# Seven block products for eight in a feature-axis transform: layer 1, blocks 0 to 2

## The chip, the cores and the metric

The kernel runs on one core of one Trainium2 chip. The metric is the device time of one execution in microseconds (us). Before the change it is 1423.32 us, the median of three runs that lie between 1423.19 and 1423.43.

The engines are named as in the profile: PE is the matrix engine (PEld its weight loads), DVE the vector engine, ACT the scalar engine, POOL the general one, and SP the engine that issues this kernel's DMAs. Each engine works through its own instructions in the order in which they were written, and waits where a semaphore is not there yet.

## The reference

Two layers, each an FNet mixing step and an MLP mixer block. x is 2048 by 512 in fp32, the MLP is 1376 wide.

```python
def _A_ref(x, dft_seq_re, dft_seq_im, dft_hid_re, dft_hid_im):
    a = jnp.einsum("bsd,ed->bse", x, dft_hid_re)
    b = jnp.einsum("bsd,ed->bse", x, dft_hid_im)
    return jnp.einsum("ts,bse->bte", dft_seq_re, a) - jnp.einsum("ts,bse->bte", dft_seq_im, b)
...
x = A_x
x = x + _A_ref(_layernorm(x, axis=-1), A_dft_seq_re, A_dft_seq_im, A_dft_hid_re, A_dft_hid_im)
x = x + _B_ref(_layernorm(x, axis=-1), B_w1, B_w2, B_w3, B_w4)
x = x + _A_ref(_layernorm(x, axis=-1), A_dft_seq_re, A_dft_seq_im, A_dft_hid_re, A_dft_hid_im)
x = x + _B_ref(_layernorm(x, axis=-1), B_w1, B_w2, B_w3, B_w4)
```

The change concerns the feature-axis transform (`dft_hid_re`, `dft_hid_im`) of the second `_A_ref`. The kernel does the two transforms in the other order: first along the sequence, then along the features.

## The kernel before, in words

Every product is made of three matmuls (`mm3`, L293 to L296). Each operand is split into a high part, which is its cast to fp32r (made by ACT), and a low part, which is what the cast lost (a subtraction on DVE). The three matmuls are high by high, high by low of the right operand, and low of the left operand by high. So the third matmul of a product is the first that needs the left operand's low part.

A mixing step goes through the 2048 rows in four blocks c = 0 to 3 of 512 rows (four tiles of 128). A block has two phases:

- `x_phase`, 16 steps. Step 2k ("plain") has 12 matmuls of 128x512 on a piece of the sequence matrix (`ws`, 512 KB), step 2k+1 ("one") has 6 on the difference of the piece's two halves. Called x0, x0', x1, x1', up to x7, x7' below.
- `y_phase`, 16 items of 12 matmuls each; each works on a sum of two pieces. Called y0 to y15 below.

What the sequence transform of a block yields (four tiles of 128x1024: re0, re1, im0, im1) needs a few sums and is then transformed along the features. For block c - 1 this happens inside the x phase of block c: eight calls of `hid`, 12 matmuls of 128x512 each, put before the steps that the table `HAT` names. The right operand of each is a 512 KB piece of the feature matrix (`hs`). `add_y` adds the sums from PSUM to the residual rows. The sums that come before (`im1-`, `re1+` and so on), and the highs and lows of the four tiles (`high`, `low`), stand in the table `late` and are issued at numbered steps of the x phase by `run_late`.

All right operands come through one stream. A piece is loaded by SP into one of four raw buffers (two more, when `state["wide"]` is set, for the pieces of a y phase: from x step 11 to the end of y). Then it becomes a slot of a ring of four: ACT casts the high part (L240, L243, L247), DVE subtracts for the low part (L257). A "one" step has a difference made on DVE first (L242), and a y item a sum (L246). A slot is made ahead, as soon as PE is done with the slot that stood in the same place. A raw buffer comes free as soon as ACT and DVE have read it, which is ahead of PE's use. The stream's loads, casts, lows and sums stand on each engine in the order of use, and between them stands what `late` and the hooks issue at the same step.

Ahead of layer 1 stands layer 0's MLP, which goes through two pairs of blocks (`by_pairs`). In the second pair (`pair == 1`, `next_too`; its main loop is at 614.7 to 687.0 us of the profile) a list `bg` of small steps is worked off by `one`, between the matmuls.

The functions that the change touches:

Of the kernel before, what the change touches and what calls it, by code (L numbers as in the profile page):

```python
# [13 lines left out]
P = 128  # L14
# [25 lines left out]
HORDER = ((1, 0), (0, 1), (1, 1), (0, 0))  # L40


@with_exitstack
def spectral_mlp_kernel(ctx: ExitStack, tc: tile.TileContext, x, ws, hs, w1, w2, w34, out):
# [17 lines left out]
    w3e = dram.tile([P, 2, CH], F32, name="w3e")  # L62
    w4s = [dram.tile([P, 4, 2, 2 * P], F32, name=f"w4s{i}") for i in range(NF // 2)]
# [39 lines left out]
    rr = [[re0[0], re1[0]], [im0[0], im1[0]]]  # L103
    rg = [[at(f"rg{i}{g}", RR + (4 * i + g) * 2 * CH, 2, CH) for g in range(KD)] for i in range(2)]
    ring, ringf = zip(*(both(f"ring{i}", RNG + i * 4 * CH, 2, 2, CH) for i in range(RING)))
    raw_at = [at(f"raw{i}", RAWS + i * 2 * CH, 2, CH, dtype=F32) for i in range(RAW)]
    raw_at += [at(f"raw{RAW + i}", word, 2, CH, dtype=F32) for i, word in enumerate((EXT + 4 * D, STG))]

# [52 lines left out]

    for layer in range(LAYERS):
        for c in range(NC):
# [29 lines left out]
    raws, slots, sums = {}, {}, {}  # L193
    held = {i: None for i in range(len(raw_at))}
    state = {"wide": False, "dma": 0, "one": 0, "two": 0, "use": 0, "made": 0, "done": 0, "limit": 0, "load": w_pieces[0]}
# [11 lines left out]
    def issue_dma(upto=None):  # L207
        while state["dma"] < (state["load"] if upto is None else upto):
# [12 lines left out]
            raws[i] = raw_at[r]  # L221
# [5 lines left out]
    def stage_one():  # L227
# [3 lines left out]
        issue_dma()  # L231
        if dest is None:
# [18 lines left out]
    def stage_two():  # L251
        n = state["two"]
        kind, ids, (a, b), _ = items[n]
        dest = slots[n]
# [6 lines left out]
    def room():  # L261
        n = state["one"]
        if n >= min(len(items), state["limit"]):
            return False
        if items[n][3] is not None:
# [16 lines left out]
    def stream():  # L282
# [150 lines left out]
    re0s, re1s, im0s, im1s = (f[:, :, 1] for _, f in (re0, re1, im0, im1))  # L433
    mid = [rr[i // 2][i % 2].rearrange("p t r (h d) -> p (t r h) d", h=2) for i in range(4)]
# [52 lines left out]
    def x_phase(c, hook):  # L487
        h = 0
        for k in range(NP):
            first, last = k == 0, k == NP - 1  # L490
            while c and h < NP and HAT[h] == k:
# [9 lines left out]
            hook(2 * k)  # L501
            mm_half(PC, ax[k][:, 2], s[:, 0], first, last)
            mm_half(PB, ax[k][:, 1], s[:, 1], first, last)
            if last:
                for i in range(2):
                    nc.scalar.copy(im1s[:, i], PC[i])
                for i in range(2):
                    nc.scalar.copy(re1s[:, i], PB[i])
            s = stream()
            run_late(2 * k + 1)  # L510
            hook(2 * k + 1)
            mm_half(PA, ax[k][:, 0], s[:, 0], first, last)
# [1419 lines left out]
```

## Time and profile before

| what | before |
|---|---|
| median of three runs | 1423.32 us |
| the profiled execution's own time | 1423.03 us |
| its span in the profile | 1421.1 us |
| PE busy | 1415.4 us |
| DVE busy | 1187.0 us |
| ACT busy | 743.0 us |
| mean DMA rate | 216 GB/s |
| x phase of layer 1, block 1 (times from the span's start) | 798.85 to 853.25 us |
| x phase of block 2 | 896.77 to 951.17 us |
| x phase of block 3 | 994.69 to 1049.09 us |

The span is the time that the profile's instructions cover. It is 1.9 us shorter than the execution's own time. PE's matmuls are pipelined: each takes 389 ns from start to end at 512 columns, but the next one starts 227 ns after it. So what counts on PE is the distance from start to start. A "busy" PE that is never idle can still be waited for by others; where PE itself waits, the profile lists it by line, with the engine that it waited for.

### The profile page before, as it was taken

The page shows a single profiled execution, that of the slowest core. Times are in us where ns is not written, and L with a number is a line of the kernel's source. Part 1 is how long each engine was busy: PE and PEld are TensorE (multiplying, and loading weights), DVE is VectorE, ACT ScalarE, POOL GpSimd, SP SyncE. Part 2 cuts the span into 40 slices and gives each one's busy share as a digit, 9 for nine tenths or more (in the row PEclk, how much of TensorE's full clock was granted, in tenths as well). Part 3 has the DMA queues.
Part 4 walks back from the last instruction along what each step waited for, and adds up shares of the span by engine and source line. Part 5 has one row for each costly group of instructions (what it writes and reads, how often), then busy time and mean ns, then how long its engine had stood idle before and what let it go on. Part 6 is the DMA issues. An engine that isn't in the chain of part 4 may idle for free.

```text
span 1421.1 us, 17861 instructions
## 1 busy us (share of the span) xinstructions
PE 1415.4 (100%) x6465; PEld 1180.1 (83%) x6465; DVE 1187.0 (84%) x1675; ACT 743.0 (52%) x1007; POOL 77.7 (5%) x105
## 2 busy tenths in 40 slices
PE   9999999999999999999999999999999999999998
PEld 7888888888888888888888888888888888899887
DVE  7986998988979888656789989889899788896676
ACT  6663464455566754434555544554555566453351
POOL 2100000000002000000000000000000020000000
PEclk9999999999999999999999999999999999999999
DMA  7867647659754857945556476575696456676864
GB/s 253 279 208 234 210 152 262 193 163 309 238 164 109 294 195 266 354 159 178 196 174 222 152 253 212 158 265 176 193 304 229 134 148 237 202 244 228 311 207 158
DMA packets 136488, 306.31 MB, mean 216 GB/s; under 512 B 9680, under 2 KB 58064, under 8 KB 133712
## 3 DMA queue, kind: packets, MB, share of 16 engines
q1 hardware_dynamic: 136400, 305.17, 65.1%
q8 instruction: 51, 0.84, 0.2%
q14 instruction: 37, 0.30, 0.1%
HBM read 250.87 MB, written 54.26 MB: 215 GB/s over the span
## 4 chain that ended last, share of the span: by engine, by line
PE 93%; DVE 4%; ACT 1%; issue 1%; POOL 0%; DMA 0%; DVEq 0%; ACTq 0%; POOLq 0%
PE psd L294 10%; PE psd L296 10%; PE psd L295 9%; PE psa L296 8%; PE psa L294 8%; PE psa L295 8%; PE psb L296 7%; PE psc L295 7%; PE psc L296 7%; PE psb L294 7%; PE psb L295 7%; PE psc L294 7%; DVE rest L480 0%; ACT tmp L342 0%; DVE ring L257 0%
## 5 line engine op out<-in xcount | busy, mean ns | idle before, releaser
L240 ACT CAST ring<-raw 128x1024 fp32r<-128x1024 f32 x127 | 133.3, 1054 | 78.5 <-PE psd L296 42.9
L257 DVE TENSOR_TENSOR ring<-raw,ring 128x1024 fp32r<-128x1024 f32 x126 | 153.5, 1220 | 13.1 <-ACT ring L240 13.0
L294 PE MATMUL psd<-ring,rr 128*128 128x512 f32 x208 | 80.9, 389 | 0.0
L295 PE MATMUL psd<-ring,rr 128*128 128x512 f32 x208 | 80.9, 389 | 0.0
L296 PE MATMUL psd<-ring,rr 128*128 128x512 f32 x208 | 80.9, 389 | 0.0
L334 POOL TENSOR_TENSOR rs<-ve,mhalf 128x4 f32<-128x4 f32 x16 | 26.9, 1683 | 723.8 <-DVE nm L333 723.8
L247 ACT CAST ring<-ring0f 128x1024 fp32r<-128x1024 f32 x28 | 29.6, 1057 | 50.7 <-DVE ring0f L246 50.7
L257 DVE TENSOR_TENSOR ring<-ring1f,ring 128x512 fp32r<-128x512 f32 (+1 forms) x56 | 53.3, 952 | 0.7 <-ACT ring L243 0.7
L313 POOL TENSOR_TENSOR rs<-ve,mhalf 128x2 f32<-128x2 f32 (+2 forms) x33 | 28.8, 872 | 415.7 <-DVE nb L312 415.7
L342 ACT ACTIVATE tmp<-xs,nb,rs 128x512 f32<-128x512 f32 x56 | 43.5, 814 | 14.6 <-POOL nb L314 14.6
L294 PE MATMUL psc<-ring,ay 128*128 128x512 f32 x128 | 49.8, 389 | 0.0
L295 PE MATMUL psc<-ring,ay 128*128 128x512 f32 x128 | 49.8, 389 | 0.0
L296 PE MATMUL psc<-ring,ay 128*128 128x512 f32 x128 | 49.8, 389 | 0.0
L294 PE MATMUL psb<-ring,ay 128*128 128x512 f32 x128 | 49.8, 389 | 0.0
L295 PE MATMUL psb<-ring,ay 128*128 128x512 f32 x128 | 49.8, 389 | 0.0
L296 PE MATMUL psb<-ring,ay 128*128 128x512 f32 x128 | 49.8, 389 | 0.0
L294 PE MATMUL psa<-ring,ay 128*128 128x512 f32 x126 | 49.0, 389 | 0.0
L295 PE MATMUL psa<-ring,ay 128*128 128x512 f32 x126 | 49.0, 389 | 0.0
L296 PE MATMUL psa<-ring,ay 128*128 128x512 f32 x126 | 49.0, 389 | 0.0
L294 PE MATMUL psd<-ring,ay 128*128 128x512 f32 x126 | 49.0, 389 | 0.0
L295 PE MATMUL psd<-ring,ay 128*128 128x512 f32 x126 | 49.0, 389 | 0.0
L296 PE MATMUL psd<-ring,ay 128*128 128x512 f32 x126 | 49.0, 389 | 0.0
(826 smaller groups left out, 4494.4 us busy)
## 6 DMA issues: line engine op xcount, KB each, us to landing
raw<-in_ws SPq DMA_DIRECT2D x183, 512.0 KB, 5.1
raw<-in_hs SPq DMA_DIRECT2D x56, 512.0 KB, 3.6
w4r<-w4d SPq DMA_DIRECT2D x44, 512.0 KB, 4.5
w3b<-w3d SPq DMA_DIRECT2D x10, 1792.0 KB, 8.9
w3d<-w3b SPq DMA_DIRECT2D x5, 1792.0 KB, 6.9
x1d<-tmp SPq DMA_DIRECT2D x12, 512.0 KB, 6.4
xs<-x1d SPq DMA_DIRECT2D x12, 512.0 KB, 5.0
w4d<-w4in SPq DMA_DIRECT2D x11, 512.0 KB, 4.7
```

The source lines that it names most:

```text
L240: nc.scalar.copy(dest[:, a:b, 0], r[0][:, a:b])
L247: nc.scalar.copy(dest[:, :, 0], lo)
L257: nc.vector.tensor_tensor(lo, src, hi.bitcast(F32), op=ALU.subtract)
L294: nc.tensor.matmul(o, lh, rh, start=first, stop=False, skip_group_check=more)
L295: nc.tensor.matmul(o, lh, rl, start=False, stop=False, skip_group_check=more)
L296: nc.tensor.matmul(o, ll, rh, start=False, stop=last, skip_group_check=more)
L313: nc.gpsimd.tensor_tensor(rs[:, :n], ve[:, :n], mhalf[:, 0, :n], op=ALU.pow)
L334: nc.gpsimd.tensor_tensor(rs, ve, mhalf[:, :, :2], op=ALU.pow)
L342: nc.scalar.activation(o, s, AF.Identity, bias=mr[2], scale=mr[1])
```

## The change

In layer 1, for blocks 0 to 2 (so in the x phases of blocks 1, 2 and 3), the feature transform is taken as a product of 2 by 2 blocks, and is done with seven block products for eight, in the manner of Strassen and Winograd. Each product (`hid7`) has 24 matmuls of 128x256 and stands before one of the steps of the new table `HAT7`. They are called h0 to h6 below, so h0 stands before x1', h1 before x2', h2 before x3', h3 before x4', h4 before x5, h5 before x6 and h6 before x7.

The left operands ("forms") are the tiles and four sums of them. Each form gets its high part by ACT into one of two places (`hf`) and its low part by DVE (`form_low`), at the step ahead of its product. `hid7_out` adds each product's result to the residual rows: six additions of 512 columns, and one of 1024. The eight casts and lows of `hs` pieces, and the four highs and lows of the tiles, go.

The right operands are seven forms of the feature matrix, the same for all blocks, 1 MB each in split form (2 pieces of 512 KB). They are made once, in layer 0's second MLP pair: `hs_forms` gives four quarters of steps (2 loads of 256 KB, then 4 sums, 7 casts, 7 lows and 7 stores of 256 KB each), which are zipped into `bg`. In layer 1 they are loaded into the raw buffers and used from there by PE with no further work. The entry "over" in `uses` says that such a buffer is free only when PE has used it. All six raw buffers are in use in these x phases too.

Besides: `w4_bring` loads into `w4_sumf`, since the sixth raw buffer's place is in use; the statistics of the rows (`y_stats`), their loads and stores are issued at other steps; in block 3 the transposes ahead of the MLP are issued later in the y phase.

```diff
+HAT7 = (3, 5, 7, 9, 10, 12, 14)
...
+    hsd = [[dram.tile([P, 2, CH], F32, name=f"hsd{i}{j}") for j in range(2)] for i in range(7)]
...
+    def form_items(step):
+        for h in range(7):
+            if HAT7[h] == step:
+                for j in range(2):
+                    item("form", piece(hsd[h][j]), dest=hsd)
+                    y_pieces.add(len(pieces) - 1)
...
             for k in range(NP):
-                if c:
+                if c and layer:
+                    form_items(2 * k)
+                elif c:
                     for h in range(NP):
                         if HAT[h] == k:
                             item("plain", piece(hs[HORDER[h % 4]]))
                 p = piece(ws[c, k][:, 2:4])
                 item("plain", p)
+                if c and layer:
+                    y_pieces.add(p)
+                    form_items(2 * k + 1)
                 item("one", p, span=(0, 1))
...
-            uses.setdefault(i, []).append((n, "two" if it[0] == "plain" else "one"))
+            uses.setdefault(i, []).append((n, {"plain": "two", "form": "over"}.get(it[0], "one")))
...
         if i and items[i - 1][3] is None:
             state["done"] += 1
-        state["use"] += 1
+        state.update(use=i + 1, over=i)
         prefetch()
         while state["two"] <= i:
             stage_two()
+        if items[i][0] == "form":
+            return raw_in[place[items[i][1][0]]]
         return slots.pop(i)
...
+    forms = [(a11, a11f), (a22, a22f), s2, (a21, a21f), s3, (a11, a11f), (a12, a12f)]
+
+    def form_high(n):
+        nc.scalar.copy(hf[n % 2], forms[n][1])
+
+    def form_low(n):
+        lo, src = forms[n]
+        nc.vector.tensor_tensor(lo, src, hf[n % 2].bitcast(F32), op=ALU.subtract)
...
+    def hid7(n):
+        ps, (lo, _) = PD[n % 2], forms[n]
+        new = n in (0, 1, 3, 6)
+        for h in range(2):
+            s = stream()
+            for i in range(2):
+                j = 2 * h + i
+                for q in range(2):
+                    v = slice(q * P, (q + 1) * P)
+                    first = new and not (j or q)
+                    o = ps[:, q * DH : (q + 1) * DH]
+                    mm3(o, hf[n % 2][:, j, v], lo[:, j, v], s[:, i, 0], s[:, i, 1], first, True, not first)
...
+        if tiles:
+            for i, f in (
+                (0, form_sum(im1s, im1s, re1s)),
+                (0, form_sum(im1s, im1s, X1, ALU.add)),
+                (1, lambda: form_high(0)),
+                (1, form_sum(s3[1], a11f, a21f)),
+                (2, lambda: form_low(0)),
+                (2, form_sum(re1s, re1s, t[:, 0:2], ALU.add)),
+                (3, form_sum(re0s, re0s, t[:, 0:2], ALU.add)),
+                (3, form_sum(re0s, re0s, t[:, 2:4], ALU.add)),
+                (4, lambda: form_high(1)),
+                (4, form_sum(s2[1], a22f, s3[1])),
+                (4, form_sum(a21f, a21f, a22f, ALU.add)),
+                (4, lambda: form_low(1)),
+                (5, lambda: form_high(2)),
+                (5, form_sum(a11f, a12f, s2[1])),
+                (6, lambda: form_low(2)),
...
+                (8, lambda: form_low(3)),
+                (8, lambda: form_high(4)),
+                (9, lambda: form_low(4)),
...
+                (13, lambda: form_low(6)),
+            ):
+                late.setdefault(i, []).append(f)
+            return
...
+            def out(i, n, src=None):
+                t, src = fp[i][0], raw[i] if src is None else src
+                act(t[:, :, 0], src)
+                nc.vector.tensor_tensor(t[:, :, 1], src, t[:, :, 0].bitcast(F32), op=ALU.subtract)
+                nc.sync.dma_start(places[n][0].rearrange("p i (l w) -> p i l w", l=2), t.bitcast(F32))
...
+                bg += [lows("t4"), *early]
+                bg[: len(work)] = [do_both(*fg) for fg in zip(bg, work)]
```

The order of the instructions shows what this does on two engines. First DVE, from the start of the x phase of block 1, before. The names: `rr11f` is im1, `rr01f` re1 and `rr00f` re0 (`rr11`, `rr01`, `rr00` their split forms), L480 is a sum, L441 a low of one of these tiles, L257 a low of a ring slot, L242 the difference for a "one" step.

```order
L480 TENSOR_TENSOR rr11f_167<-rr11f_167,rr01f_165 128x2x512
L257 TENSOR_TENSOR ring0_176<-raw3_187,ring0_176 128x2x512
L480 TENSOR_TENSOR rr01f_165<-rr01f_165,tmp_107 128x2x512
L242 TENSOR_TENSOR ring2f_181<-raw0_184 128x512
L257 TENSOR_TENSOR ring1_178<-raw0_184,ring1_178 128x2x512
L480 TENSOR_TENSOR rr11f_167<-rr11f_167,tmp_107 128x2x512
L441 TENSOR_TENSOR rr01_164<-rr01f_165,rr01_164 128x2x512
L257 TENSOR_TENSOR ring2_180<-ring2f_181,ring2_180 128x512
L257 TENSOR_TENSOR ring3_182<-raw1_185,ring3_182 128x2x512
L480 TENSOR_TENSOR rr00f_161<-rr00f_161,tmp_107 128x2x512
L441 TENSOR_TENSOR rr11_166<-rr11f_167,rr11_166 128x2x512
```

And the same place after the change. `imLf` holds im0 and im1, `reLf` re0 and re1; L552 is a sum, L479 the low part of a form, L285 a low of a ring slot, L266 the difference for a "one" step.

```order
L285 TENSOR_TENSOR ring0_200<-raw0_208,ring0_200 128x2x512
L552 TENSOR_TENSOR s3f_189<-imLf_183 128x1024
L266 TENSOR_TENSOR ring1f_203<-raw0_208 128x512
L479 TENSOR_TENSOR imL_182<-imLf_183,hf0_190 128x4x256
L552 TENSOR_TENSOR reLf_185<-reLf_185,tmp_121 128x1024
L285 TENSOR_TENSOR ring1_202<-ring1f_203,ring1_202 128x512
L285 TENSOR_TENSOR ring2_204<-raw1_209,ring2_204 128x2x512
L552 TENSOR_TENSOR reLf_185<-reLf_185,tmp_121 128x1024 x2
L266 TENSOR_TENSOR ring3f_207<-raw1_209 128x512
L552 TENSOR_TENSOR s2f_187<-reLf_185,s3f_189 128x1024
L552 TENSOR_TENSOR imLf_183<-imLf_183,reLf_185 128x4x256
L479 TENSOR_TENSOR reL_184<-reLf_185,hf1_191 128x4x256
```

Of the seven lows of forms, the first (`imL`, for h0) and the second (`reL`, for h1) stand here; ahead of the second stand all sums of the re tiles and two sums of forms (`s2f`, and the one into `imLf`), where before these tiles' sums and lows were spread over steps 1 to 6.

Second DVE, further on in the same x phase, after the change: from the low of x5 (from buffer `raw0`) on, with the lows for h3 (`imL`) and h4 (`s_`, here `s3`) and the low of x6 (from `raw1`).

```order
L285 TENSOR_TENSOR ring2_204<-raw0_208,ring2_204 128x2x512
L266 TENSOR_TENSOR ring3f_207<-raw0_208 128x512
L285 TENSOR_TENSOR ring3_206<-ring3f_207,ring3_206 128x512
L479 TENSOR_TENSOR imL_182<-imLf_183,hf1_191 128x4x256
L552 TENSOR_TENSOR tmp_121<-tmp_121,psd0_286 128x2x256
L285 TENSOR_TENSOR ring0_200<-raw1_209,ring0_200 128x2x512
L479 TENSOR_TENSOR s3_188<-s3f_189,hf0_190 128x1024
```

Before the change the same stretch, from the difference for x5' on, has no low of a left operand (the first row is the low of an `hs` piece, the others belong to x5, x5' and the next `hs` piece):

```order
L257 TENSOR_TENSOR ring3_182<-raw3_187,ring3_182 128x2x512
L242 TENSOR_TENSOR ring1f_179<-raw0_184 128x512
L257 TENSOR_TENSOR ring0_176<-raw0_184,ring0_176 128x2x512
L257 TENSOR_TENSOR ring1_178<-ring1f_179,ring1_178 128x512
L257 TENSOR_TENSOR ring2_180<-raw1_185,ring2_180 128x2x512
```

So the lows of h3 and h4 now stand behind the lows of the pieces x5 and x6 in DVE's order, although PE uses h3 ahead of x5 and h4 ahead of x5.

Third SP, the loads of the same stretch, before. What a row waits for stands behind it: `DVE_49` is a wait for DVE, `DMAHW` one for an earlier DMA.

```order
L222 DMA raw2_186<-in_hs 128x1024 [waits DMAHW2_49,DVE_49]
L222 DMA raw3_187<-in_hs 128x1024 [waits DMAHW3_49,DVE_49]
L222 DMA raw0_184<-in_ws 128x1024 [waits DMAHW5_49,DVE_49]
L222 DMA raw1_185<-in_hs 128x1024 [waits DMAHW6_49,DVE_49]
L222 DMA raw2_186<-in_hs 128x1024 [waits DMAHW4_49,DMAHW0_49,DVE_49]
```

And after. `rawr0` and `raw0` are one buffer under two names, and so for the others; `hsd30` and `hsd31` are the two pieces of h3, and so on; `PE_49` is a wait for PE.

```order
L243 DMA rawr1_215<-hsd30_95 128x1024 [waits DMAHW1_49,DMAHW2_49,DVE_49,Activation_49]
L243 DMA rawr4_218<-hsd31_96 128x1024 [waits PE_49]
L243 DMA rawr5_219<-hsd40_97 128x1024 [waits DMAHW3_49,PE_49]
L224 DMA tmp_121<-x2d_78 128x2x512 [waits DMAHW4_49]
L243 DMA rawr3_217<-hsd41_98 128x1024 [waits DMAHW0_49,DMAHW5_49,DVE_49,Activation_49]
L243 DMA raw0_208<-in_ws 128x1024 [waits DMAHW6_49,PE_49]
L243 DMA rawr2_216<-hsd50_99 128x1024 [waits DMAHW7_49,PE_49]
L243 DMA rawr0_214<-hsd51_100 128x1024 [waits DMAHW6_49,DVE_49,Activation_49]
L243 DMA raw1_209<-in_ws 128x1024 [waits DMAHW1_49,PE_49]
```

Here the load of x5 (`raw0`) waits for the last matmul of h2's first half, which reads `rawr0`, and that of x6 (`raw1`) for the last matmul of h3's first half, which reads `rawr1`. Before, no load of a piece for these x phases waited for PE. In the x phases of blocks 2 and 3 the buffers have other numbers, and x5 and x6 wait for the same two halves.

More of the change, by code (lines that the diff above doesn't have):

```diff
@@ L103, in spectral_mlp_kernel @@
     rr = [[re0[0], re1[0]], [im0[0], im1[0]]]
+    (imL, imLf), (reL, reLf) = (both(f"{n}L", RR + i * 4 * CH, 4, CH) for i, n in enumerate(("im", "re")))
+    s2, s3 = (both(f"s{n}", RR + word * CH, 4, DH) for n, word in ((2, 8), (3, 10)))
+    hf = [at(f"hf{i}", RR + (12 + 2 * i) * CH, 4, DH) for i in range(2)]
     rg = [[at(f"rg{i}{g}", RR + (4 * i + g) * 2 * CH, 2, CH) for g in range(KD)] for i in range(2)]
@@ L191, in spectral_mlp_kernel @@
         for i in it[1]:
-            uses.setdefault(i, []).append((n, "two" if it[0] == "plain" else "one"))
-    raws, slots, sums = {}, {}, {}
+            uses.setdefault(i, []).append((n, {"plain": "two", "form": "over"}.get(it[0], "one")))
+    raws, slots, sums, place = {}, {}, {}, {}
     held = {i: None for i in range(len(raw_at))}
-    state = {"wide": False, "dma": 0, "one": 0, "two": 0, "use": 0, "made": 0, "done": 0, "limit": 0, "load": w_pieces[0]}
+    state = {"wide": False, "dma": 0, "one": 0, "two": 0, "use": 0, "over": 0, "made": 0, "done": 0, "limit": 0, "load": w_pieces[0]}
     x_left = [(0, 1), (1, 1)] + [(j, 2) for j in range(2, NT, 2)]
@@ L231, in stage_one @@
         issue_dma()
+        if kind == "form":
+            state["one"] += 1
+            return
         if dest is None:
@@ L253, in stage_two @@
         kind, ids, (a, b), _ = items[n]
+        if kind == "form":
+            state["two"] += 1
+            issue_dma()
+            return
         dest = slots[n]
@@ L1835, in hook @@
                             f(7)
+                if layer and c:
+                    if k < 2:
+                        rows((pairs[1], X1)[k], x1d, (c - 1) * TC + (2, 0)[k], 2, False)
+                    if c < NC - 1:
+                        return
+                    if k in (0, 1):
+                        for j in (2 * k, 2 * k + 1):
+                            normed_act(tmp[:, j], xt(j), ln2[j])
+                    if k in (1, 2):
+                        for q in (2 * k - 2, 2 * k - 1):
+                            turn_one(turned0, q, tmp[:, q])
+                    if k == 3:
+                        turn_out(turned0)
+                    if k == NP - 1:
+                        turn_in(ztf[0])
+                    return
                 if k == 1 and c:
```

130 lines of the change are left out of this document (114 added, 16 removed).

## The prediction

> **What bounds the kernel now.** I read the page's busy times and PE's waits first.
>
> ```profile
> PE 1415.4 (100%) x6465; PEld 1180.1 (83%) x6465; DVE 1187.0 (84%) x1675; ACT 743.0 (52%) x1007; POOL 77.7 (5%) x105
> PE psd L139 <- POOL mhalf L55: 1.4, 1, 1.4
> PE psb L426 <- DVE rr L339: 0.2, 1, 0.2
> ```
>
> PE is busy for 1415.4 of 1421.1 us, and its two waits (the list of waits has no more) come to 1.6 us, the longest 1.4. So time goes only with PE's work, and every wait of PE is added whole. What a matmul costs is its distance to the next, which the view by windows gives: the three x phases of blocks 1 to 3, and a stretch of layer 1's MLP with nothing but matmuls of 256 columns (columns: window, its length, then busy time and count for PE, PEld, DVE, ACT, POOL).
>
> ```profile
> 798.85:853.25 54.40, 54.40 (x242) 45.05 (x240) 47.01 (x58) 26.90 (x32) 2.83 (x2) 1.00 0.69 229
> 896.77:951.17 54.40, 54.40 (x242) 45.05 (x240) 47.01 (x58) 26.90 (x32) 2.83 (x2) 1.00 0.70 229
> 994.69:1049.09 54.40, 54.40 (x242) 45.05 (x240) 47.02 (x58) 28.24 (x34) 2.83 (x2) 1.00 0.74 248
> 1255.20:1310.70 55.50, 55.50 (x469) 55.46 (x468) 45.32 (x65) 26.88 (x42) 0.00 (x0) 1.00 0.70 228
> L294 PE MATMUL psb<-un,hr 128*128 128x256 f32 x50 | 14.1, 283 | 0.0
> ```
>
> 54.40 us over 240 weight loads (one for each matmul; the window's edges cut two more matmuls) is 0.2267 us for 512 columns; 55.50 over 468 is 0.1186 for 256. The granted clock is 1.00 throughout.
>
> **What the seven products give.** A block had 8 x 12 = 96 matmuls, 96 x 0.2267 = 21.76 us. It now has 7 x 24 = 168 matmuls of half the width, 168 x 0.1186 = 19.92. That is 1.84 less for a block, 5.5 for three: 0.39%, no more, and only if PE waits for nothing new. The Trainium skill (TensorE: Matmul & The Clock Gate, Back-to-back issue gap) gives an isolated warm matmul N/2.4 + 2.5 ns, 215.8 and 109.2 here; by that the estimate would be 96 x 0.2158 - 168 x 0.1092 = 2.4 us a block. The trace's distances are longer at both widths, and decide.
>
> So what matters is whether the left operands' lows are there in time. I lay the rows of the changed order end to end with durations of this trace. DVE's at the start of block 1's x phase, with ACT's casts and two groups:
>
> ```profile
> 799.05 0.69 DVE L242 TENSOR_TENSOR ring3f<-raw 128x512 f32<-128x512 f32 x1 [1.31 <-PE psa L296]
> 802.90 1.22 DVE L257 TENSOR_TENSOR ring<-raw,ring 128x1024 fp32r<-128x1024 f32 x1 [0.28 <-ACT ring L240]
> 804.04 1.22 DVE L480 TENSOR_TENSOR rr01f<-rr01f,tmp 128x1024 f32<-128x1024 f32 x1
> 805.85 0.69 DVE L242 TENSOR_TENSOR ring2f<-raw 128x512 f32<-128x512 f32 x1 [0.59 <-PE psb L296]
> 806.46 1.22 DVE L257 TENSOR_TENSOR ring<-raw,ring 128x1024 fp32r<-128x1024 f32 x1
> 806.63 0.62 ACT L243 CAST ring<-ring2f 128x512 fp32r<-128x512 f32 x1 [0.28 <-DVE ring2f L242]
> L240 ACT CAST ring<-raw 128x1024 fp32r<-128x1024 f32 x14 | 14.7, 1054 | 10.5 <-PE psd L296 5.5 <-PE psb L296 3.6 <-ACT ring L240 1.2
> L296 PEld LDWEIGHTS psd<-ring,rr x32: 187/188/188, 807.2 to 844.6; 128*128 128x128 f32 x32
> L294 PE MATMUL psd<-ring,rr 128*128 128x512 f32 x32 | 12.4, 389 | 0.0
> ```
>
> A DVE row of 1024 elements takes 1.22 us, and the next starts 1.14 after it (802.90 to 804.04); one of 512 takes 0.69, the next 0.60 later (805.85 to 806.46). ACT's casts take 1.05 and 0.62; ACT starts 0.09 after DVE's end (805.85 + 0.69 to 806.63). A weight load is 0.19, and a matmul ends 0.39 - 0.23 = 0.16 after the next has started. DVE's waits for PE in these rows show that it already works at PE's heels here.
>
> **h0 and h1: DVE's queue.** Time 0 is the phase's start, 798.85. PE does x0 (12 matmuls, 2.72), x0' (1.36), x1 (2.72), then h0. Its third matmul is the first to read the low part: wanted at 6.80 + 2 x 0.12 = 7.04. DVE has, in order: the difference for x1' (starts 0.20), two sums of im1, low x1', low x2 (it needs x0's end on PE, then ACT's cast: 4.05, as at 802.90), s3, the difference for x2', low of h0. 4.05 + 1.14 + 1.14 + 0.60 = 6.93, plus 1.22 and the weight load: 8.34. PE waits 1.3 us. Then h1: PE goes on with 22 matmuls (2.61), x1' and x2 (4.08) and wants the low at 8.34 + 6.69 + 0.24 = 15.27. DVE, from 8.07: sum of re1, low x2', low x3, two sums of re0, difference for x3', s2, the sum into a21, low of h1; seven rows of 1.14 (the last ends 0.08 later) and two of 0.60 make 9.26 and end at 17.33, with the weight load 17.52. PE waits 2.25. Nothing covers this, since DVE has no gap there that the sums could use. Before, the same sums had up to twice the time, and lows of tiles were due later.
>
> **h2: 0.7.** The difference for x4' needs the ring place that x2' leaves (0.16), then 0.69, cast 0.62, low 0.60, the form's low 1.22, weight load 0.19 and hand-overs of 0.2: 3.7, against x3 and two matmuls (2.96).
>
> **h3 and h4: the raw buffers.** A form's buffer is freed by PE, not by DVE. The load of x5 waits for the end of h2's first half; the low of x5 stands ahead of the low of h3 on DVE; h3 comes ahead of x5 on PE. So between the end of h2's first half and h3's third matmul PE has only h2's second half 1.42, x3' 1.36, x4 2.72 and 0.24: 5.74 us. In that time must fit the landing L, cast 1.05, low x5 1.14, difference 0.69, cast 0.62, low x5' 0.60, h3's low 1.22, weight load 0.19, and hand-overs of 0.2: L + 5.7. PE waits L. For h4 it is the load of x6, freed by h3's first half, whose low stands ahead of h4's: L + 1.05 + 1.14 + 1.22 + 0.19 + 0.1 = L + 3.7, against 1.42 + 1.36 + 0.24 = 3.02: PE waits L + 0.7. Before, no such load waited for PE; SP's longest waits were for DVE. For L, the list of DMA issues and the view of the stream's line (all loads of the window 796 to 856):
>
> ```profile
> SPq L222 <- DVE ring L257: 37.9, 14, 5.6
> raw<-in_ws SPq DMA_DIRECT2D x183, 512.0 KB, 5.1
> raw<-in_hs SPq DMA_DIRECT2D x56, 512.0 KB, 3.6
> DMA to landing us min/median/max: 3.3/4.6/9.5
> ```
>
> I take 3.6, the row of the pieces that are loaded amid an x phase: these loads too start when little else is under way, since the queue behind them waits for PE. The bounds are 3.3 and 4.6. So h3 waits 3.6, h4 4.3.
>
> **h5, h6 and the y phase.** h5's low has 24 x 0.12 + 2.72 + 1.36 = 6.9 us after h4's and needs 0.69 + 0.62 + 0.60 for x6', 4 x 0.34 for a weight's sums, 0.60 for a result and 1.22: 5.1, so it costs nothing. h6's low stands behind y0's sum, which needs the ring place that x6 leaves: 0.16 + 1.14 + 1.22 + 0.19 = 2.7 against x6' and 0.24: 1.1. With L = 4.6 two loads one after the other (x7, then y0 in the same buffer) make 2 x 4.6 + 5.0 = 14.2, against 12.7 of PE: 1.5. In the y phases nothing is added between PE and its slots: 0, at most 0.5 in block 3, where DVE was busy for 42.8 of 43.6 us:
>
> ```profile
> 1049.00:1092.60 43.60, 43.60 (x194) 36.09 (x193) 42.81 (x41) 24.60 (x29) 0.00 (x0) 1.00 0.76 247
> ```
>
> **Layer 0's second pair.** It gains 44 DVE rows of 256 columns and 28 casts, and 28 stores and 8 loads of 256 KB.
>
> ```profile
> 614.70:687.00 72.30, 72.30 (x320) 59.89 (x319) 48.55 (x89) 33.99 (x53) 3.57 (x8) 1.00 0.44 150
> L480 DVE TENSOR_TENSOR w4sumf<-w4raw 128x256 f32<-128x256 f32 x2 | 0.8, 418 | 0.0
> ```
>
> DVE has 48.55 us of work in 72.30; 44 x 0.34 (0.42 less the overlap of 0.08) adds 15.0, which leaves 8.8 free, and ACT and the DMAs have half their time. The matmuls hide it: 0. If one step's seven rows end last somewhere, 7 x 0.42 = 2.9. It adds only, so no gain.
>
> **The sum.** A block: 1.3 + 2.25 + 0.7 + 3.6 + 4.3 + 1.1 = 13.25 of waits, less 1.84: 11.4. Blocks 1 to 3 have the same order and the same dependences: 34.2. On the profiled execution's 1423.0 (span 1421.1 and 1.9 around it; the median is 0.3 above): 1457.2, so 1457. With L = 3.3: 3 x 10.8 = 32.4, 1455; with L = 4.6: 3 x (15.6 - 1.8) = 41.5, plus 0.5 and 2.9: 1468.
>
> **The rivals.**
>
> *Only DVE's queue counts.* If the loads of x5 and x6 come early enough after all, h3 waits like h2 (0.7) and h4 not at all: 6.05 - 1.84 = 4.2 a block, 12.6 in all: 1435.6. If the short waits at h2, h3 and h6 vanish too (2.5 a block), 1428. For it: DVE's order needs no DMA to come out. Against it: the order's rows make those loads wait for PE. Chance 0.13.
>
> *All waits are covered, and it is faster.* DVE's total in an x phase hardly grows (it loses 12 lows of 1024 and four sums of 512, and gains 12 rows of 1024 and six of 512: 1.2 us of 54.4). If DVE did two of the sums before the phase's start, where it waits 1.31 us for PE (row 799.05), and came to h1 3.55 us sooner than I laid it, and the pieces x5 and x6 were in SBUF by then, PE would never wait: 1423.0 - 5.5 = 1417.5. It decides at h1: each us that is missing there costs 3, so with 1.8 us missing the gain is gone. Against it: DVE's rows have one order, and the sums stand behind the difference for x1', which waits for PE. Chance 0.07.
>
> *The clock falls in the long waits.* No wait of before is over 1.4 us, and there the granted clock stays 1.00; h3's and h4's would be 3.6 and 4.3. If matmuls after them ran at twice their distance for as long as one product (24 x 0.1186 = 2.85), six such waits add 17: 1474; four of the six, 1469. The Trainium skill (TensorE: Matmul & The Clock Gate, Part 1) has PE at half clock after an idle window of about 3.4 us, until it was busy for as long; by this the estimate is up to 1.7 us lost for each wait, 10 in all. It also has the window run freely, so that waits of 3.6 and 4.3 us would seldom cover a whole one. No run here shows it so far. Chance 0.10.
>
> **How the numbers follow.** Forecast 0.67 (1455 to 1468), only DVE's queue 0.13, faster 0.07, clock 0.10, and 0.03 that gain and waits cancel within 0.2% (2.8 us; less could hardly be told from no change). The range must take in the forecast with L's bounds and DVE's case, and the clock's lower part: 1428 to 1469. Faster 0.07, same 0.03, slower 0.90.
>
> **What would show it.** Right: PE's list of waits names the forms' lows (`imL`, `reL`, `s2`, `s3`), 11 to 15 us for each x phase of blocks 1 to 3 with the longest ahead of h4; these phases last some 65.8 us for 54.4; SP's loads of x5 and x6 wait for PE. Wrong: an x phase of about 52.6 us without waits of PE (faster), or one of 58.6 with waits at h0 and h1 alone. A granted clock under 1.00 in these phases is the third rival. PE's waits in layer 0's second pair should be none.

## The result, and the profile after

The changed kernel takes 1502.08 us (median of four runs, 1496.98 to 1503.56); the kernel before took 1423.26 beside it. The ratio is 1.0548 (95%: 1.0521 to 1.0574). The sign was as forecast, but the time lies outside the range. The profiled execution took 1500.71 us, its span is 1498.6: 77.5 us more than before. By stages (ends from the timeline of PE; the two profiled executions):

| stage | before | after | more |
|---|---|---|---|
| layer 0, second MLP pair | 107.60 | 126.28 | 18.7 |
| x phases of blocks 1, 2, 3 | 3 x 54.40 | 72.95, 70.78, 75.47 | 56.0 |
| y phases of blocks 1, 2 | 2 x 43.52 | 44.75, 44.77 | 2.5 |
| all else | | | 0.3 |

The page's busy times:

```profile
PE 1436.8 (96%) x6681; PEld 1200.9 (80%) x6681; DVE 1205.8 (80%) x1725; ACT 733.4 (49%) x1020; POOL 74.5 (5%) x105
```

PE's list of waits, without the two rows that stood there before (1.4 and 0.4 us here; columns: what waits and for whom; us in total, times, the longest):

```profile
PE psd L330 <- DVE s L479: 14.2, 6, 5.1
PE psd L330 <- DVE reL L479: 13.2, 6, 4.5
PE psd L330 <- DVE imL L479: 11.8, 6, 2.9
PE psd L328 <- ACT hf L475: 3.6, 6, 1.1
PE psa L328 <- DVE rest L552: 3.5, 2, 3.3
PE psd L328 <- DVE rest L552: 2.9, 2, 1.8
PE psd L328 <- ACT rest L1303: 2.0, 1, 2.0
PE psa L328 <- ACT rest L1303: 1.2, 1, 1.2
PE psd L330 <- DVE h L750: 1.2, 1, 1.2
PE psc L328 <- ACT h L760: 0.7, 1, 0.7
PE psd L328 <- DVE tmp L552: 1.9, 2, 0.9
```

The first four rows are the x phases: 42.8 us in 24 waits, for the forms' lows (L479) and highs (L475). L330 is the third matmul of a product, the one that the forecast named. The six rows below them are the second pair, 11.5 us in 8 waits, for sums and copies that empty PSUM banks. The last row is the y phases.

Waits don't carry all of it. The windows of the pair, of the three x phases, and of a stretch right behind the longest wait (columns as before: PE, PEld, DVE, ACT, POOL, then the granted clock):

```profile
615.00:741.30 126.30, 114.64 (x475) 91.42 (x474) 90.20 (x180) 58.82 (x106) 6.94 (x12) 0.96 0.65 223
817.80:890.75 72.95, 59.06 (x313) 51.24 (x312) 47.12 (x53) 23.36 (x29) 0.00 (x0) 0.93 0.61 198
935.50:1006.28 70.78, 57.97 (x313) 50.24 (x312) 47.12 (x53) 23.42 (x29) 0.00 (x0) 0.95 0.61 195
1051.05:1126.52 75.47, 59.38 (x313) 51.70 (x312) 47.11 (x53) 23.39 (x29) 0.00 (x0) 0.93 0.64 212
864.00:868.40 4.40, 4.40 (x22) 4.40 (x22) 3.63 (x8) 2.61 (x3) 0.00 (x0) 0.50 0.60 165
```

The 22 matmuls of the last window (two of them cut by its edges) start 0.21 us apart, for 0.1186 at full clock, and the clock column says 0.50. So the 56.0 us of the x phases are: 42.8 of waits, 24 x 0.16 = 3.8 because the last matmul ahead of a wait runs to its end, less 5.5 of gain; what is left, 14.9, is slower matmuls. Of these 10.9 stand in the timeline as matmuls at about twice their distance behind seven of the waits (1.2 to 2.4 us behind each); most of the rest is the first matmul after a wait, 0.10 longer to the next one than its neighbours. In the pair it is 11.5 of waits, 8 x 0.16 = 1.3, and 5.9 slower, 4.1 of them at twice the distance behind two waits (2.5 and 1.6).

How one wait comes about, h4 of block 1. PE's timeline (start, length; in brackets the idle time ahead of it), DVE's, SP's issues (a row's time is that of the first of the x issues in it), and ACT's row in its list of waits for the three blocks:

```profile
858.15 0.28 PE L329 MATMUL psd<-rawr,hf 128*128 128x256 f32 x1
863.57 0.58 PE L330 MATMUL psd<-rawr,s 128*128 128x256 f32 x1 [5.13 <-DVE s L479]
```

```profile
861.15 1.22 DVE L285 TENSOR_TENSOR ring<-raw,ring 128x1024 fp32r<-128x1024 f32 x1 [6.69 <-ACT ring L264]
862.29 1.22 DVE L479 TENSOR_TENSOR s<-s3f,hf 128x1024 fp32r<-128x1024 f32 x1
880.01 1.23 DVE L270 TENSOR_TENSOR ring0f<-raw,raw 128x1024 f32<-128x1024 f32 x1 [4.44 <-DMA raw<-in_ws]
881.16 1.22 DVE L479 TENSOR_TENSOR reL<-reLf,hf 128x1024 fp32r<-128x1024 f32 x1
```

```profile
855.40 0.33 SPq L243 DMA_DIRECT2D raw<-in_ws  x1
875.00 12.17 SPq L243 DMA_DIRECT2D raw<-in_ws  x7
```

```profile
ACT ring L264 <- DMA raw<-in_ws: 46.5, 9, 8.0
```

SP can issue the load of x6 only at 855.40, when PE has done with h3's first half, which lay in that buffer. ACT waits for the landing, DVE waits 6.69 us for ACT's cast, does the low of x6 at 861.15, and only then the low of h4 (862.29), which PE wants at 858.4. DVE had nothing to do in these 6.69 us but to hold its place in the queue. The same happens at h6: a load issued at 875.00 (just as DVE's low of x7 ends, at 874.98), a sum for y0 that waits for it until 880.01, and behind it the low of h6.

The second pair, where the forecast had no waits. SP's issues, then in the timelines DVE's first row of the forms' sums and one of ACT's casts, and the row of those casts in ACT's list of waits:

```profile
630.87 0.39 SPq L942 DMA_DIRECT2D w3b<-w3d  x1
631.31 0.42 SPq L1195 DMA_DIRECT2D hsr<-in_hs  x1
```

```profile
640.98 0.43 DVE L552 TENSOR_TENSOR hp01f<-hsr,hsm 128x256 f32<-128x256 f32 x1 [5.37 <-issue]
```

```profile
679.55 0.41 ACT L1199 CAST hp<-hsr 128x256 fp32r<-128x256 f32 x1 [5.50 <-DMA hsd<-hp]
```

```profile
ACT hp L1199 <- DMA hsd<-hp: 10.4, 5, 5.5
```

DVE waits 5.37 us at the head of its queue for a load of 256 KB that was issued right behind the 1.8 MB load of `w3b`; that small load landed 9.6 us after its issue. ACT waits five times, 10.4 us in all, for a store out of `hp` to be over before it may write `hp` again. Behind these rows stand the sums and copies that empty PE's PSUM banks.

### The profile page after: what moved, and what is told of

It reads as the page before. It is cut to its first block, busy times and chain, and to the rows that moved or that the text cites. A ratio compares the mean times of both kernels' runs of the same rounds, so it can differ in the third digit from the quotient of the medians.

```text
span 1498.6 us, 18501 instructions
## 1 busy us (share of the span) xinstructions
PE 1436.8 (96%) x6681; PEld 1200.9 (80%) x6681; DVE 1205.8 (80%) x1725; ACT 733.4 (49%) x1020; POOL 74.5 (5%) x105
## 4 chain that ended last, share of the span: by engine, by line
PE 81%; DVE 9%; DMA 5%; ACT 3%; issue 2%; SPq 0%; POOL 0%; DVEq 0%; ACTq 0%; POOLq 0%
PE psd L330 9%; PE psd L328 8%; PE psd L329 8%; PE psa L330 7%; PE psa L329 7%; PE psa L328 7%; PE psb L330 6%; PE psb L329 6%; PE psb L328 6%; PE psc L329 6%; PE psc L330 6%; PE psc L328 6%; DMA raw<-in_ws 3%; DVE ring L285 2%; DMA hsd<-hp 1%
## 5 line engine op out<-in xcount | busy, mean ns | idle before, releaser
L264 ACT CAST ring<-raw 128x1024 fp32r<-128x1024 f32 x103 | 107.9, 1051 | 108.6 <-DMA raw<-in_ws 48.5
L285 DVE TENSOR_TENSOR ring<-raw,ring 128x1024 fp32r<-128x1024 f32 x102 | 124.1, 1219 | 41.6 <-ACT ring L264 41.5
L285 DVE TENSOR_TENSOR ring<-ring1f,ring 128x512 fp32r<-128x512 f32 (+1 forms) x56 | 53.3, 951 | 5.2 <-ACT ring L267 5.1
L328 PE MATMUL psd<-rawr,hf 128*128 128x256 f32 x168 | 53.1, 316 | 3.6 <-ACT hf L475 3.6
L329 PE MATMUL psd<-rawr,hf 128*128 128x256 f32 x168 | 52.2, 310 | 0.0
L285 DVE TENSOR_TENSOR ring<-ring3f,ring 128x1024 fp32r<-128x1024 f32 (+1 forms) x50 | 49.2, 984 | 2.8 <-ACT ring L267 2.4
L330 PE MATMUL psb<-ring,ay 128*128 128x512 f32 x128 | 49.8, 389 | 0.0
L330 PE MATMUL psc<-ring,ay 128*128 128x512 f32 x128 | 49.8, 389 | 0.0
L330 PE MATMUL psd<-ring,ay 128*128 128x512 f32 x126 | 49.0, 389 | 0.0
L330 PE MATMUL psa<-ring,ay 128*128 128x512 f32 x126 | 49.0, 389 | 0.0
```

Source lines behind the costliest of these rows:

```text
L264: nc.scalar.copy(dest[:, a:b, 0], r[0][:, a:b])
L285: nc.vector.tensor_tensor(lo, src, hi.bitcast(F32), op=ALU.subtract)
L328: nc.tensor.matmul(o, lh, rh, start=first, stop=False, skip_group_check=more)
L329: nc.tensor.matmul(o, lh, rl, start=False, stop=False, skip_group_check=more)
L330: nc.tensor.matmul(o, ll, rh, start=False, stop=last, skip_group_check=more)
```

## The experiments

The theory behind them: the time goes to three things, each to be had by itself. The lows of the forms stand too late on DVE (x phases); the making of the right operands holds up DVE and ACT through its transfers (pair); and behind a wait the clock falls. The rivals: that the pair's excess is the added rows themselves; that the clock's part comes only with long waits; and that the products' order or their operands cost more than the waits show.

### The forms made, and not used

Layer 1 is that of before; layer 0's pair still makes and stores the right operands.

```diff
-                if c and layer:
-                    form_items(2 * k)
-                elif c:
+                if c:
...
-            x_phase(c, hook, layer and c, tiles)
+            x_phase(c, hook)
```

> The change's forms are made in layer 0's second MLP pair, but layer 1 is the one of before, and nobody reads them. Theory: the pair alone costs what its stage of the changed kernel's trace shows, 126.3 us against 107.6 of before, so this kernel takes 1423.3 + 18.7 = 1442 (1439 to 1445), with waits of PE for sums of PSUM banks (DVE and ACT standing before a DMA's landing), about 11.7 us, and some 6 us more because matmuls run slower after the long ones. Rival, as the prediction had it: the sums are hidden, and the pair is late only through what layer 1 loads; then 1423 to 1426.

Measured: 1440.99 us (1440.45 to 1443.47), ratio 1.0124 (1.0107 to 1.0140). PE's list of waits has rows for the pair alone besides the old one of 1.4 us; the three largest:

```profile
PE psd L323 <- DVE rest L547: 4.8, 3, 1.9
PE psa L323 <- DVE rest L547: 4.5, 3, 3.3
PE psd L323 <- ACT rest L1298: 2.7, 1, 2.7
```

So the pair costs 17.9 us by itself, as the theory has it, and the rest is layer 1's.

### The lows of h3 to h6 ahead of the steps that wait

The forms' highs and lows are issued at other steps: h3's low no longer stands behind the low of x5, nor h4's behind that of x6. A second thing changes with it: the results of h3 to h6 are added right behind each product.

```diff
+                if ready[-1] in (3, 4, 5, 6):
+                    hid7_out(ready.pop())
...
+                (5, lambda: form_high(3)),
                 (6, lambda: form_low(2)),
-                (7, lambda: form_high(3)),
-                (8, lambda: form_low(3)),
-                (8, lambda: form_high(4)),
-                (9, lambda: form_low(4)),
-                (10, lambda: form_high(5)),
-                (11, lambda: form_low(5)),
-                (12, lambda: form_high(6)),
-                (13, lambda: form_low(6)),
+                (6, lambda: form_low(3)),
+                (7, lambda: form_high(4)),
+                (8, lambda: form_low(4)),
+                (9, lambda: form_high(5)),
+                (10, lambda: form_low(5)),
+                (10, lambda: form_high(6)),
+                (12, lambda: form_low(6)),
```

> The changed kernel with the lows of h3 to h6 issued earlier, ahead of the lows of x5 and x6 on DVE, and the results of h3 to h6 added as soon as they are there. The loads of x5 and x6 still wait for PE as before. Theory (the order on DVE makes h3 and h4 wait for two transfers): the waits at h3 and h4, 3.6 and 4.5 us a block in the changed kernel's trace, fall under 1.5 each, those at h0 and h1 (1.2 and 2.3) stay, the clock falls less often, and the x phases go from about 73 to 60 to 63 us: 1502 - 33 = 1469 (1460 to 1478). Rival (DVE has too much to do in these phases, whatever its order): the waits move to x5, x6 and h5, the phases stay above 70 us and the time above 1492.

Measured: 1470.67 us (1470.48 to 1472.02), ratio 1.0335 (1.0320 to 1.0351): 31.4 less than the changed kernel. The windows of its x phases:

```profile
816.50:878.65 62.15, 56.39 (x313) 48.51 (x311) 45.14 (x51) 21.56 (x27) 0.00 (x0) 0.97 0.63 206
923.20:985.75 62.55, 56.38 (x313) 48.59 (x311) 45.13 (x51) 21.55 (x27) 0.00 (x0) 0.97 0.63 205
1030.30:1093.90 63.60, 55.87 (x313) 48.27 (x311) 45.21 (x51) 21.54 (x27) 0.00 (x0) 0.97 0.67 226
```

and the rows of the forms' lows in PE's list of waits there:

```profile
PE psd L330 <- DVE imL L479: 8.5, 6, 3.3
PE psd L330 <- DVE reL L479: 5.6, 5, 1.4
PE psd L330 <- DVE s L479: 1.0, 3, 0.3
```

The wait for `s` falls from 14.2 to 1.0 and the x phases from 219.2 to 188.3 us. So it was the place in DVE's queue that decided at h3 and h4. What is left at h0 and h1 (1.0 and 0.5 + 1.4 us in each block) is DVE's own work, as forecast. But part of the wait moved on: h5, which waited for nothing in the changed kernel, now waits 0.98, 1.18 and 3.30 us (the rest of the `imL` row), and h6 still 0.63 in two blocks. On DVE the low of h5 stands behind the low of x6, and now behind the addition of h4's result too, the second thing changed. In block 3 ACT casts x6 at 1071.69, as soon as its load, issued at 1065.35, has landed. So a late load still counts there, one product further on: the rival holds in this part. All three phases are still slower than the 54.40 of before.

### A wait with nothing else: the low of x4 five times, and eight times

In the kernel before, the low of x4 is computed five or eight times over in blocks 1 to 3 of layer 1 (the same values each time). It makes three waits of PE and changes nothing else.

```diff
+    again = set()
...
+                if layer and c and k in (4,):
+                    again.add(len(items))
...
-        nc.vector.tensor_tensor(lo, src, hi.bitcast(F32), op=ALU.subtract)
+        for _ in range(5 if n in again else 1):
+            nc.vector.tensor_tensor(lo, src, hi.bitcast(F32), op=ALU.subtract)
```

Five times:

> The kernel before, with the low of x4 in the x phases of blocks 1 to 3 of layer 1 subtracted five times over instead of once (same operands, same result). A measure of a wait of PE by itself: four more rows of 1.14 us on DVE, 4.6 us, less the slack that DVE has there. Both theories: three waits of the same length, 2 to 3.5 us each, and 1423.3 + 3 times that, 1430 to 1434. Waits this short should leave the clock alone.

Measured: 1436.68 us (1436.50 to 1437.20), ratio 1.0095 (1.0080 to 1.0110). Longer than expected. PE's row in the list of waits, its timeline behind the first of the three, and two windows there:

```profile
PE psc L299 <- DVE ring L261: 8.0, 3, 2.7
```

```profile
829.23 0.79 PE L299 MATMUL psc<-ring,ax 128*128 128x512 f32 x1 [2.65 <-DVE ring L261]
829.82 0.63 PE L300 MATMUL psc<-ring,ax 128*128 128x512 f32 x1
830.24 0.63 PE L298 MATMUL psc<-ring,ax 128*128 128x512 f32 x1
```

```profile
829.23:832.64 3.41, 3.41 (x8) 2.73 (x9) 3.41 (x6) 0.00 (x0) 0.00 (x0) 0.50 0.54 159
832.64:836.05 3.41, 3.41 (x16) 2.80 (x16) 3.36 (x10) 1.32 (x2) 2.10 (x2) 1.00 0.58 162
```

After 2.65 us of waiting the matmuls come 0.42 us apart instead of 0.2267, at a granted clock of 0.50, until 832.64; after that it is back. The same behind the other two. The span is 13.6 longer: 8.0 of waits, 3 x 0.16 = 0.5, and 5.1 from the clock, 1.7 us for each wait. The expectation that waits this short leave the clock alone is refuted.

Eight times:

> The same with eight times. Three more rows of 1.14 us in each of three places, so if a wait costs its length and no more, it takes 3 x 3.4 = 10.3 us more than the one with five times. If the clock falls in waits this long (6 to 7 us) and matmuls then run at half speed for some us, each of the three costs 1.2 to 2.4 us on top, as after the waits of 3.7 to 5.1 us in the changed kernel: 14 to 17.5 us more than with five times, and the granted clock below 1.00 right after each wait.

Measured: 1449.26 us (1448.92 to 1449.62), ratio 1.0183 (1.0168 to 1.0198). PE's row of waits, and a window behind the first:

```profile
PE psc L299 <- DVE ring L261: 19.3, 3, 6.4
```

```profile
833.10:837.40 4.30, 4.30 (x11) 3.29 (x10) 4.27 (x12) 0.00 (x0) 0.19 (x1) 0.50 0.51 159
```

The span is 25.8 longer: 19.3 of waits, 0.5, and 6.0 from the clock, 2.0 for each. So a wait 2.4 times as long costs hardly more clock: the price is one of about 2 us for each wait (2.5, 1.9 and 1.7 here). In all it takes 12.6 more than with five times, between the two sums of the expectation: 11.3 are waits, and the clock's part is small because the waits with five times had paid it already.

### The pair without its stores, and without its DMAs

Both stand on the kernel that makes the forms and doesn't use them. The first leaves out the 28 stores (so nothing waits for a store); the second also leaves out the loads of quarters 2 to 4, all quarters being computed from the first one's pieces.

```diff
-                nc.sync.dma_start(places[n][0].rearrange("p i (l w) -> p i l w", l=2), t.bitcast(F32))
...
-                nc.sync.dma_start(r, places[0][2])
+                if n == 0:
+                    nc.sync.dma_start(r, places[0][2])
```

Without the stores:

> As the kernel with unused forms (1441.0), but the 28 stores of the forms are left out, so the forms are never in DRAM. In the changed kernel's trace ACT waits five times for such a store before it may cast into the same buffer again, 10.4 us in all, and DVE waits 7.9 us for the loads of pieces of the feature matrix. If transfers at the head of the two queues make the pair's 17.9 us, leaving out the stores takes away over half: 1428 to 1434. If the casts, lows and sums themselves make it, leaving out the stores changes little: 1437 to 1441.

Measured: 1429.74 us (1429.58 to 1430.27), ratio 1.0048 (1.0032 to 1.0065). Without the loads too:

> The same, and the loads of the second to fourth quarter are left out too: all four quarters work on the first one's pieces, with the same 44 rows on DVE and 28 casts on ACT. If only transfers cost, nothing is left: 1423 to 1427. If the added rows cost by standing between a PSUM bank's result and the addition that frees the bank (DVE waits for ACT's cast, ACT for DVE's sum), 5 us or more stay: 1428 to 1435.

Measured: 1427.99 us (1427.78 to 1428.38), ratio 1.0035 (1.0022 to 1.0049). What is left of PE's waits, besides two of 0.2 and the old one of 1.4:

```profile
PE psc L323 <- ACT h L755: 1.3, 1, 1.3
PE psd L325 <- DVE h L745: 1.3, 1, 1.3
```

Each against the kernel before beside it, the excess is 17.9 us, then 6.8, then 5.0. So leaving out the stores takes 11.1 away, leaving out the loads 1.8 more, and 5.0 stays with the rows themselves, which delay a `h` of the MLP by 1.3 us twice (with the two of 0.2 that is 3.0 of the 5.0; the rest was not traced). Neither pure case holds: mostly the transfers, with a rest of rows. The 11.1 is not ACT's waits alone. The stores also stand on SP ahead of the loads: without them the second quarter's second load is issued at 628.15 instead of 631.33, and DVE waits 1.4 us for it instead of 5.4. These runs don't divide the 11.1 between the two.

### The waits for the left operands taken away

On the version with the lows ahead, the products take weights that have lain in SBUF all along as their left operands, so no product can wait for a form. The forms are still made; the values that come out are not the transform's.

```diff
-        ps, (lo, _) = PD[n % 2], forms[n]
+        ps = PD[n % 2]
...
-                    mm3(o, hf[n % 2][:, j, v], lo[:, j, v], s[:, i, 0], s[:, i, 1], first, True, not first)
+                    w = ay[j + 4][:, q]
+                    mm3(o, w[:, 0, v], w[:, 1, v], s[:, i, 0], s[:, i, 1], first, True, not first)
```

> The kernel with the lows of h3 to h6 ahead (1470.7), but the seven products take weights of the sequence transform for the left operands, so no product waits for its own form; the products' values are not those of the transform. All work of DVE, ACT and the DMAs is still there. Theory: the waits for the lows at h0 to h6 go (about 5 us a block), with them most of the lost clock, and an x phase without waits takes 144 x 0.2267 + 168 x 0.1187 = 52.6 us. Some waits stay where a product must wait for the addition that empties its bank. So 53 to 57 us a phase in blocks 1 and 2, and 1441 + 3 times -1.8 to +2: 1440 to 1452. Rival (the right operands, loaded straight for PE, come late by themselves): PE waits for the loads of the forms, and the phases stay near 60 us: 1465 or more.

Measured: 1460.80 us (1460.19 to 1462.83), ratio 1.0268 (1.0253 to 1.0284). Longer than expected. The first x phase, and the waits of the three blocks:

```profile
817.90:875.65 57.75, 53.34 (x313) 46.86 (x311) 45.04 (x51) 21.46 (x27) 0.00 (x0) 1.00 0.66 220
```

```profile
PE psc L328 <- ACT imLf L595: 5.5, 2, 2.7
PE psd L328 <- DVE tmp L553: 5.3, 3, 2.0
PE psc L328 <- ACT rr11f L595: 5.0, 1, 5.0
```

No product waits for a form. But banks of PSUM are now emptied too late: PE waits for ACT's copies out of them (L595), which stand on ACT behind casts of sums that wait for PE, and for an addition on DVE. The first phase is still 3.4 us longer than before, where the pure count of matmuls would make it 1.8 shorter. Its two waits of 1.72 and 2.72, twice 0.16 and the 52.6 of the count make 57.4 of the 57.75, so the products' order and operands cost hardly anything beside the waits. What is late is another row of the same queues.

### The lows ahead, and the pair's loads ahead

The version with the lows ahead, with the load of a quarter's second piece issued in one step with the first's, ahead of the load of `w3b`.

```diff
-                    work[n : n + 2] = [do_both(*work[n : n + 2])]
+                    work[n : n + 3] = [do_both(work[n], do_both(*work[n + 1 : n + 3])), lambda: None]
```

> The kernel with the lows of h3 to h6 ahead (1470.7), and in layer 0's second pair the load of a quarter's second piece issued right behind the first, ahead of the 1.8 MB of weights that stood between them on SP. In the changed kernel's trace that piece landed 9.6 us after its issue once, and DVE waited 5.4 us for it, PE 3.3 for DVE. Theory: this wait goes, and with it the clock that fell after it: 3 to 6 us less, 1465 to 1468. Rival (the loads are late however they are ordered): 1469 to 1472.

Measured: 1466.26 us (1464.13 to 1471.27), ratio 1.0309 (1.0289 to 1.0329). The pair is 3.5 us shorter (121.60 for 125.09), and DVE's wait for that load is gone. Three of the four runs lie below all of the version with only the lows ahead, and the fourth (1471.27) among them. By the median it is the best of the versions that compute the whole, and it is slower than the kernel before: none was found that beats it.

## Why the prediction was wrong

**The gain** was right in size. With no wait in their way the 24 matmuls of a product are 0.1197 us apart, for 0.1186 of the estimate.

**The waits of the left operands** were right in place and nearly in size. With the 0.16 of the running-out matmul, measured for blocks 1, 2 and 3 (forecast in brackets): h0 1.2, 1.2, 1.2 (1.3); h1 2.3, 2.3, 2.3 (2.25); h2 0.6, 0.6, 0.6 (0.7); h3 3.6, 3.8, 4.4 (3.6); h4 5.3, 3.8, 4.3 (4.3); h5 0 (0). At h1 and h3 a part of it is a wait for the form's high on ACT (0.5 at h1, 0.4 to 1.1 at h3), which the forecast left out; the low ends the wait all the same. Moving the lows of h3 and h4 took their waits away, so the cause is shown too.

**h6 was mis-sized**: 1.1, measured 2.3, 2.5, 4.7. The forecast had the load for y0 there in time and put its delay at the bound (1.5). In the trace that load is issued at 875.00, just as DVE's low of x7 ends, and landed by 880.01, and this decides. Together the waits are 15.2, 14.1 and 17.4 a block for 13.25: 6.9 us more in three blocks.

**Layer 0's second pair is the first step that failed.** "The matmuls hide it: 0", with a bound of 2.9; it is 18.7 here and 17.9 by itself. The working compared DVE's busy time with the stretch, and the DMAs' share with what was free. But an in-order engine is not held up by the sum of its rows, but by one row at its head that waits. The rows that do wait are visible in the change: a cast into a buffer that a store still reads, a sum of a piece whose load was issued one place behind a big one. Without the stores, and the delay that they put on the loads, 11.1 us go. Even the rows alone cost 5.0, where the bound said 2.9 at most.

**The clock is the second.** It had a chance of 0.10, as a case of its own, and it happened: 10.9 us of half-speed matmuls in the x phases and 4.1 in the pair, out of 20.8 (14.9 + 5.9) that slower matmuls cost in all. The rival's price (2.85 for each of four to six long waits) was too high for one wait and its number too low: nine waits were followed by it, at 1.2 to 2.5. One argument against it was that no run showed it. But the kernel before has no wait over 1.4 us, so a forecast of two waits of 3.6 and 4.3 in each block lay outside what its trace covers. And its wait of 1.4, at the start of the program, did not leave the matmuls at full speed, as the prediction read it: the 24 behind it start 0.213 us apart up to 4.5 us and 0.112 from then on, though the clock column says 1.00 there.

The rule weighed there, of the Trainium skill (TensorE: Matmul & The Clock Gate, Part 1), has the half clock follow an idle window of about 3.4 us that runs freely, so that shorter waits can't fill one. The window that runs freely agrees with these traces: the clock changes only on steps of 3.413 us (last section). But the window need not be idle throughout: waits of 2.65 us were enough three times of three. Its other half agrees: the slow stretch behind the first of them lasted 3.41 us (829.23 to 832.64).

**The y phases** were given 0 to 0.5; they are 2.5 longer. In blocks 1 and 2 the first accumulation into `psd` waits 0.94 for the addition that empties h6's bank, which stands on DVE behind the statistics of the rows (`y_stats`).

Added up: 34.2 forecast, 6.9 more in the x phases' waits, 14.9 for slower matmuls there, 18.7 for the pair, 2.5 for the y phases: 77.2 of the 77.5. Either of the two failed steps would have put the time outside the range alone: without the pair's 18.7 it is 1482, without the 14.9 it is 1486.

What stays open: whether a version in which nothing waits would reach the 1417.5 of the count of matmuls. The nearest, with the left operands given, still waits for banks, and was not brought further.

## What to carry to other kernels

When a change puts rows into in-order queues, don't compare sums of busy time: go through the added rows one by one, ask what each waits for (a landing, a store out of the buffer that it writes, a bank), and charge what stands behind it on that engine for that wait. A buffer that PE frees instead of DVE puts the next load, with all of its 4 to 5 us, on PE's own path, unless the rows that PE wants next stand ahead of the rows that use the load. Where a forecast has PE waiting in a place where it never did, charge the clock too, by what these traces show: 1.7 us or a little more for each wait over 3 us, half of that on average for one of 2 to 3 us, and take two waits close together as one.

## What the runs showed of the hardware

The clock after a wait. Two waits of the same length in the changed kernel, in blocks 1 and 2, both at h3: 2.92 us, up to 853.92, is not followed by the half clock, and 2.93 us, up to 971.80, is. The windows around them are cut at steps of 3.413 us:

```profile
848.79:852.20 3.41, 1.83 (x8) 1.05 (x7) 1.99 (x3) 2.46 (x4) 0.00 (x0) 1.00 0.20 79
852.20:855.61 3.41, 1.69 (x14) 1.70 (x15) 2.26 (x3) 0.75 (x1) 0.00 (x0) 1.00 0.50 154
968.25:971.67 3.42, 0.50 (x2) 0.30 (x2) 2.74 (x5) 1.63 (x3) 0.00 (x0) 1.00 0.37 97
971.67:975.08 3.41, 3.28 (x15) 3.28 (x16) 0.67 (x2) 0.00 (x0) 0.00 (x0) 0.50 0.14 56
```

The first wait is split over two steps, in which PE is idle for 1.6 and 1.7 us; the second lies, with a short one ahead of it, in one step, idle for 2.9. This holds in all the traces. Behind the start of the program, in each of the seven traces with such stretches, all 27 of half clock begin on one grid of 3.413 us steps, counted from the trace's first, and last one step (21 of them) or two (6). The step ahead of each tells: where PE was idle for 1.96 us of it or more, the next was at half clock, 25 times of 25; for 1.65 to 1.84, 2 times of 9; for less, never. So where the wait falls on the grid counts, and not its length alone: of the waits of PE of 3.1 us or more all 12 were followed by the half clock, of those from 2.0 to 2.93 us 11 of 21. A wait of 1.44 shortly behind one of 0.53 was followed by it in 3 blocks of 9: those in which most of both fell into one step (1.65, 1.96 and 1.97 us of it). The price is that of one step at half speed, 3.41 / 2 = 1.7 us, whether the wait took 2.65 or longer. A second step came where PE was still idle for 0.88 us or more of the first (0.56 or less: one step). Where exactly between 1.65 and 1.96 us the border lies, these traces leave open.

A small load behind a big one on the same queue: 256 KB landed 9.6 us after its issue behind 1.8 MB, and 6.5 or less in the version that issues it ahead; in the changed kernel the median of the loads of L1195 is 6.1 and the fastest 4.2 (the view of that line, stretch 600 to 720 us):

```profile
DMA to landing us min/median/max: 4.2/6.1/9.6
```
